# The end of the first part of a fused attention and MLP backward kernel: order of the last two tiles

## The chip, the cores and the metric

The kernel runs on one core of one Trainium2 chip. The metric is the device time of one execution in microseconds (us). A core has TensorE (PE in the profile, with its weight loads as PEld), VectorE (DVE), ScalarE (ACT), GpSimd (POOL) and SyncE (SP, which here only issues DMAs). Every engine works through its own instructions in the order in which the program lists them, and instructions of different engines wait for each other through semaphores.

## What is computed

The reference is a block with attention (32 heads of 16) times a gate, and its gradients. S is 2048, D is 512, F is 1792. Cut to what matters:

```
xn = layernorm(x)                       # A_x
s  = attention(layernorm-ed x) @ wo
y  = layernorm(xn)
m  = gelu(y @ w1 + b1) @ w2 + b2
g  = silu(m)
out = x + s * g
# returned: out and the gradients of A_x, wqkv, wo, w1, b1, w2, b2 for a given grad_out
```

For this case only a few of the backward values count. With sg = sigmoid(m) the gate is G = m * sg, its derivative times grad_out is B = (sg + (1 - sg) * G) * grad_out, and the gradient that goes into the output projection is dso = grad_out * G. The gradient of the attention's output is dO = dso @ wo^T. G and B ("gbr"), and dso ("dsr"), are stored to DRAM for the last part; dO is needed by attention's backward in two layouts.

## The kernel before

The program has three parts. The first (class Pre, lines 102 to 469) makes everything that attention reads: the norms, q, k, v, the hidden layer of the MLP, the gate and dO. The second (attention_core) runs attention forward and backward in one sweep of 64 blocks of 16 steps, one step for each 128 keys. The third (class Grads) makes the weight gradients and the gradient of x.

The work is scheduled by hand: the order in the code is the order on every engine. Rows are handled in 16 tiles t of 128 rows. The loop at lines 425 to 457 runs over t; in each turn it works on four different tiles at different stages:

- gate(t), lines 363 to 378: PE multiplies 14 times for m (ps_m, L367), DVE adds the bias (L373), ACT takes a tanh (L374), DVE makes sg, G and dso from it (L375, L376, L377; "the gate chain" below). It hands back a function for gate_b, four POOL instructions that make B (L381 to L384). For t below 14 the loop calls it at once; for 14 and 15 it is put into the list lastb.
- dproj(t - 2), lines 389 to 394: PE makes dO of an older tile (ps_do, L392), DVE copies it to SBUF (nat, L393), POOL copies it again into another layout (ND, L394).
- t_do(t - 3): PE transposes that dO (tp_ps, L173), ACT copies the result (dOT, L177). t_ds(t - 1): the same for dso (dsoT, L177), which dproj of that tile will read.
- after(t) for every fourth tile: SP stores ND and dOT to DRAM (L403, L404) and loads from there what attention's first pair of heads needs ("do", L95 and L98), which waits for the store. gate_store(t) for every second tile: SP stores gbr and dsr of two tiles (L409, L410).

After the loop, lines 458 to 469 finish tiles 13 to 15: dproj(14), t_do(13), t_ds(15), t_do(14), dproj(15), t_do(15), after(15), then both functions in lastb on POOL, and gate_store(15) with POOL as the queue that issues its two DMAs.

In turn t = 15, line 446 is a one-element Exp on ACT. Its purpose is the load of the table that Exp needs (ACT_TABLE_LOAD) ahead of attention's first exp.

Behind lastb, POOL's next instructions are the memsets of a second set of attention operands (make_op, L47 to L50), then small copies and loads in the steps of attention.

A step g of attention has on PE: scores s (L1082) and d (L1104), the transposes tT of an older step (L1166), the products X (L1196, L1199, L1203) and, from step 20, Z (L1280). ACT takes the exp (L1091) and copies tT into ek (L1178). DVE multiplies d by the exp into gts (L1121) and copies a small share of ek (L1178). SP transposes every pair of steps of gts by DMA into gk (L1137); there are four gts tiles of two steps each. An ek tile holds four steps.

The first part's tiles give their SBUF to the tiles of attention. Tile pools with reuse_waits="tile" make the first write into a new tile wait for the last use of the old tiles that lay in the same bytes, a DMA that reads them included. The tile gd (sg, m and dsr of the last tiles, lines 341 and 342) and the tiles gbr and dOT lie in that region, and ek tiles come to lie there.

The functions that the change touches:

Of the kernel before, what the change touches and what calls it, by code (L numbers as in the profile page):

```python
# [10 lines left out]
ACT = mybir.ActivationFunctionType  # L11
ALU = mybir.AluOpType
# [4 lines left out]
NT = S // 128  # L17
# [84 lines left out]
class Pre:  # L102


    def __init__(self, ctx, tc, k, op0, A_x, A_wqkv, A_wo, B_w1, B_b1, B_w2, B_b2, grad_out):
        nc = tc.nc
# [27 lines left out]
        b2bc = sm.tile([128, D], bf16, name="b2bc")  # L134
# [10 lines left out]
        ld = nc.sync.dma_start  # L145
# [24 lines left out]
        def tp(src, dst, e):  # L170
            pt = psT.tile([128, IC, 128], bf16, name="tp_ps", tag="tp")
            for b in range(IC):
                nc.tensor.transpose(pt[:, b, :], src(b), k.ident_bf[:])  # L173
            if e:
                nc.vector.tensor_copy(out=dst, in_=pt[:])
            else:
                nc.scalar.copy(out=dst, in_=pt[:])  # L177
# [52 lines left out]
        def stores_nat(gq):  # L230
            g = gq % 2
            t0 = gq * 4
            ld(out=k.NAT_s[:, :, t0:t0 + 4, :].rearrange("a p t c -> p a t c"), in_=NS[:, g].rearrange("p a t j c -> p a t (j c)"))
            ld(out=k.NATQq_s[:, :, t0:t0 + 4, :].rearrange("a p t c -> p a t c"), in_=NQ[:, g].rearrange("p a t j c -> p a t (j c)"))
# [11 lines left out]
        def wkv_rows(ic):  # L246
            arr = yr[:, 2 * (ic % 2):2 * (ic % 2) + 2, :].rearrange("p x d -> p (x d)").rearrange("p (r h e) -> p r h e", r=8, h=4)
            for e0, f0 in ((0, 2 * D), (16, D)):
                nc.gpsimd.tensor_copy(out=arr[:, :, :, e0:e0 + 16],
                                      in_=wqkv_sb[:, ic, f0:f0 + D].rearrange("p (r h e) -> p r h e", r=8, h=4))  # L250
            nc.gpsimd.dma_start(out=k.WKV_s[ic * 128:ic * 128 + 128, :], in_=arr.rearrange("p r h e -> p (r h e)"))
# [18 lines left out]
        def bound():  # L270
            nc.vector.tensor_reduce(out=kmx[:, 4:5], in_=kmx[:, 0:4], axis=AX.X, op=ALU.max)
            nc.vector.tensor_scalar(out=kmx[:, 5:6], in0=kmx[:, 4:5], scalar1=UINFL, scalar2=None, op0=ALU.mult)
            nc.scalar.activation(out=UT, in_=qn2[:], func=ACT.Sqrt, scale=kmx[:, 5:6])
            ld(out=k.UT_s[:, :], in_=UT)
# [64 lines left out]
        gbr = mid.tile([128, 4, 2, D], bf16, name="gbr", tag="m2")  # L339
        dOT = mid.tile([128, 2, IC, 512], bf16, name="dOT", tag="m3")  # L340
        gd = mid.tile([128, 8, D], bf16, name="gd", tag="m4")
        gw, dsr = gd[:, 0:4, :], gd[:, 4:8, :]
# [6 lines left out]
        def hid(g, fc):  # L349
            ps = psA.tile([128, 512], f32, name="ps_h1", tag="mm")  # L350
            for ic in range(IC):
                nc.tensor.matmul(ps[:], lhsT=w1_sb[:, ic, fc * 128:(fc + 1) * 128], rhs=yT[:, ic, g * 512:(g + 1) * 512],  # L352
                                 start=(ic == 0), stop=(ic == IC - 1))
            nc.scalar.activation(out=hgT[:, g % 2, fc, :], in_=ps[:], func=ACT.Gelu_apprx_tanh, bias=b1c[:, fc:fc + 1], scale=1.0)
            i = (g * 7 + fc // 2) % 3
            nc.vector.tensor_scalar(out=h1r[:, i, fc % 2, :], in0=ps[:], scalar1=b1c[:, fc:fc + 1], scalar2=None, op0=ALU.add)
            if fc % 2 == 1:
                ld(out=h1v[:, fc - 1:fc + 1, g * 512:(g + 1) * 512], in_=h1r[:, i])
            if fc in (6, 13):
                c0 = fc - 6  # L360
                ld(out=hgv[:, c0:c0 + 7, g * 512:(g + 1) * 512], in_=hgT[:, g % 2, c0:c0 + 7, :])

        def gate(t):
            g, t4 = t // 4, t % 4
            ps = psA.tile([128, 512], f32, name="ps_m", tag="mm")
            for fc in range(FC):
                nc.tensor.matmul(ps[:], lhsT=hgT[:, g % 2, fc, t4 * 128:(t4 + 1) * 128], rhs=w2_sb[:, fc, :],  # L367
                                 start=(fc == 0), stop=(fc == FC - 1))
            dot = dotr[:, g % 2, t4, :]
            m_, sg = gw[:, 2 * (t % 2), :], gw[:, 2 * (t % 2) + 1, :]  # L370
            ta = tau[:]
            G_, B_ = gbr[:, t % 4, 0, :], gbr[:, t % 4, 1, :]
            nc.vector.tensor_tensor(out=m_, in0=ps[:], in1=b2bc[:], op=ALU.add)  # L373
            nc.scalar.activation(out=ta, in_=m_, func=ACT.Tanh, scale=0.5)  # L374
            nc.vector.tensor_scalar(out=sg, in0=ta, scalar1=0.5, scalar2=0.5, op0=ALU.mult, op1=ALU.add)  # L375
            nc.vector.tensor_tensor(out=G_, in0=m_, in1=sg, op=ALU.mult)  # L376
            nc.vector.tensor_tensor(out=dsr[:, t % 4, :], in0=dot, in1=G_, op=ALU.mult)  # L377
            return lambda: gate_b(B_, G_, sg, dot)

        def gate_b(B_, G_, sg, dot):  # L380
            nc.gpsimd.tensor_scalar(out=B_, in0=sg, scalar1=-1.0, scalar2=1.0, op0=ALU.mult, op1=ALU.add)  # L381
            nc.gpsimd.tensor_tensor(out=B_, in0=B_, in1=G_, op=ALU.mult)
            nc.gpsimd.tensor_tensor(out=B_, in0=B_, in1=sg, op=ALU.add)
            nc.gpsimd.tensor_tensor(out=B_, in0=B_, in1=dot, op=ALU.mult)  # L384

        def t_ds(t):
            tp(lambda b: dsr[:, t % 4, b * 128:(b + 1) * 128], dsoT[:, t % 2], 0)

        def dproj(t):
            ps = psA.tile([128, 512], f32, name="ps_do", tag="mm")  # L390
            for bc in range(IC):
                nc.tensor.matmul(ps[:], lhsT=dsoT[:, t % 2, bc, :], rhs=woT[:, bc, :], start=(bc == 0), stop=(bc == IC - 1))  # L392
            nc.vector.tensor_copy(out=ndc[:, t % 2, :], in_=ps[:])  # L393
            nc.gpsimd.tensor_copy(out=ND[:, (t // 4) % 2, :, t % 4, :], in_=ndc[:, t % 2, :].rearrange("p (a c) -> p a c", a=NPAIR))  # L394

        def t_do(t):
            g = (t // 4) % 2
            tp(lambda b: ndc[:, t % 2, b * 128:(b + 1) * 128], dOT[:, g, :, (t % 4) * 128:(t % 4) * 128 + 128], 0)

        def after(t):  # L400
            if t % 4 == 3:
                g = t // 4
                ld(out=k.NATQd_s[:, :, g * 4:g * 4 + 4, :].rearrange("a p t c -> p a t c"), in_=ND[:, g % 2])  # L403
                ld(out=k.DOT_s.rearrange("(c p) s -> p c s", p=128)[:, :, g * 512:(g + 1) * 512], in_=dOT[:, g % 2])  # L404
                op0["do"](g)

        def gate_store(t, ld=ld):
            if t % 2 == 1:
                ld(out=k.GB_s.rearrange("(t p) x d -> p t x d", p=128)[:, t - 1:t + 1], in_=gbr[:, (t - 1) % 4:(t - 1) % 4 + 2])  # L409
                ld(out=k.DSO_s.rearrange("(t p) d -> p t d", p=128)[:, t - 1:t + 1], in_=dsr[:, (t - 1) % 4:(t - 1) % 4 + 2, :])  # L410

        def load_dot(g):
            ld(out=dotr[:, g % 2], in_=go2[:, g * 4:g * 4 + 4])

        lastb = []
# [9 lines left out]
        for t in range(NT):  # L425
            g, t4 = t // 4, t % 4
            n0, n1 = (0, 4, 8, 11, 14)[t4:t4 + 2]
            if g < 3:
                for fc in range(n0, n1):
                    hid(g + 1, fc)  # L430
            if t == 4:
                op0["q"]()
            if t >= 1:
                gate_store(t - 1)
            if t == 0:
                bound()
            gb = gate(t)
            if t == 0:
                stores_nat(3)
            if t < 14:  # L440
                gb()
            else:
                lastb.append(gb)
            if t == 15:

                nc.scalar.activation(out=b2bc[0:1, 0:1], in_=b2bc[0:1, 0:1], func=ACT.Exp)
            if t >= 2:
                dproj(t - 2)
            if t >= 3:
                t_do(t - 3)  # L450
                after(t - 3)
            if t >= 1:
                t_ds(t - 1)
            if t4 == 3 and g + 2 < 4:
                load_dot(g + 2)
            if 2 <= t < 6:
                wkv_rows(t - 2)
        dproj(NT - 2)
        t_do(NT - 3)
        after(NT - 3)  # L460
        t_ds(NT - 1)
        t_do(NT - 2)
        after(NT - 2)
        dproj(NT - 1)
        t_do(NT - 1)
        after(NT - 1)
        for gb in lastb:
            gb()
        gate_store(NT - 1, nc.gpsimd.dma_start)


GA = 0.044715
# [993 lines left out]
```

## Time and profile before

| what | value |
|---|---|
| median of 3 runs | 2246.61 us (2244.68 to 2248.53) |
| span of the profiled execution, first to last instruction | 2242.4 us |
| median of the runs less that span | 4.2 us |
| PE, DVE, ACT, POOL busy in the span | 2160.1, 1912.2, 1734.5, 606.8 us |
| last matmul group of gate(15), L367 | starts at 207.0 us |
| last copy of dO by DVE, L393 | starts at 220.2 us |
| attention's first exp, L1091 | starts at 221.9 us |
| gate_b of tiles 14 and 15 on POOL, L381 to L384 | 221.6 to 230.2 us |
| table load, L446 | 1.28 us, and 0.20 us for the Exp behind it |

The page gives the span of the profiled execution and no other time of it, so the runs' median is the only figure for what lies around the span. Times within the profile are counted from the span's start. A line of a timeline reads: start, duration, engine, line of the kernel, operation, what is written and read, shape, count, and in brackets how long the engine stood idle before it and what ended that. A granted clock of 0.50 means that PE ran at half speed. A chain of waits reads: start, duration, who.

### The profile page before, as it was taken

To read this page: it belongs to the slowest core of one execution; us is meant where nothing else is said; L and a number is where in the kernel's file an instruction comes from. 1 tells how busy PE (TensorE), PEld (TensorE's weight loads), DVE (VectorE), ACT (ScalarE), POOL (GpSimd) and SP (SyncE) were. 2 spreads that over 40 slices of the span, in tenths; PEclk is the share of its full clock that TensorE was granted. 3 is DMA by queue.
4 is the path that set the end of the run, shared out by engine and by line. 5 is a ranking of instruction groups with operands and counts; after the bars stand their busy time and mean duration, and the time that the engine had idled before them with its cause. 6 is when DMAs were issued, how large, how long until landed. Compare 5 with 4: busy or idle time off the path is not lost.

```text
span 2242.4 us, 74217 instructions
## 1 busy us (share of the span) xinstructions
PE 2160.1 (96%) x30690; PEld 1205.0 (54%) x30690; DVE 1912.2 (85%) x3626; ACT 1734.5 (77%) x2481; POOL 606.8 (27%) x1387
## 2 busy tenths in 40 slices
PE   6998999999999999999999999999999999989996
PEld 3444555555555555555555555555555554434443
DVE  6676799999999999999999999999999997777623
ACT  4764788888888888888888888888888886674213
POOL 4276413122222222131222222221312224310012
PEclk9999899999999999999999999999999999999998
DMA  7786999999999999999999999999999999899972
GB/s 238 242 273 197 184 199 194 202 200 203 195 203 194 200 197 206 196 199 200 198 203 197 203 192 204 199 199 197 204 196 190 204 205 273 194 257 240 233 222 94
DMA packets 1421747, 461.15 MB, mean 206 GB/s; under 512 B 1334622, under 2 KB 1405662, under 8 KB 1421408
## 3 DMA queue, kind: packets, MB, share of 16 engines
q1 hardware_dynamic: 1406880, 424.67, 99.3%
q0 software_dynamic: 12944, 30.16, 5.4%
q8 instruction: 240, 3.93, 0.8%
q10 hardware_dynamic: 1584, 1.57, 0.2%
q14 instruction: 99, 0.81, 0.1%
HBM read 62.79 MB, written 64.75 MB: 57 GB/s over the span
## 4 chain that ended last, share of the span: by engine, by line
PE 86%; DMA 5%; DVE 2%; issue 2%; ACT 2%; POOL 2%; SPq 0%; POOLq 0%; DVEq 0%; ACTq 0%
PE tT L1166 23%; PE d L1104 14%; PE X L1196 10%; PE Z L1280 10%; PE X L1199 5%; PE X L1203 5%; PE s L1082 2%; PE ps_m L367 2%; PE ps_dy L902 2%; PE ps_dw L973 2%; PE ps_dh L868 2%; PE ps_h L352 2%; DMA out_dram<-ot 2%; PE XT L1222 1%; PE ps_dwkv L820 1%
## 5 line engine op out<-in xcount | busy, mean ns | idle before, releaser
L1121 DVE TENSOR_TENSOR gts<-d,ets 128x512 bf16<-128x512 f32 x2048 | 1363.2, 684 | 101.0 <-ACT ek L1178 20.3
L1091 ACT ACTIVATE ets<-s 128x1024 bf16<-128x1024 f32 x1024 | 1048.7, 1024 | 198.5 <-PE s L1082 95.2
L1166 PE MATMUL tT<-ident_bf,ets 128*128 128x128 bf16 x7168 | 568.9, 219 | 16.7 <-ACT ek L1178 6.9
L1166 PEld LDWEIGHTS <-ets 128*128 128x128 bf16 x7168 | 445.5, 97 | 242.0 <-issue 240.2
L1178 ACT COPY ek<-tT 128x448 f32<-128x448 f32 (+2 forms) x1024 | 501.6, 490 | 8.1 <-DVE ek L1178 6.9
L1104 PE MATMUL d<-QDT,KVT 32*128 32x512 bf16 x2048 | 458.6, 385 | 0.0
L1082 PE MATMUL s<-QDT,KVT 32*128 32x512 bf16 x2048 | 401.6, 381 | 3.4 <-ACT ets L1091 3.2
L1104 PEld LDWEIGHTS <-KVT 32*128 32x128 bf16 x2048 | 145.4, 91 | 323.9 <-issue 323.9
L1196 PE MATMUL X<-ets,NAT 128*32 128x256 bf16 x4096 | 300.6, 284 | 0.1
L1203 PE MATMUL X<-gts,NAT 128*17 128x256 bf16 x4096 | 290.0, 273 | 0.0
L1199 PE MATMUL X<-ets,Lc 128*32 128x256 bf16 x4096 | 289.9, 273 | 0.0
L1340 POOL COPY tick<-gts 1x2 bf16<-1x2 bf16 x205 | 36.2, 176 | 606.1 <-DVE gts L1121 606.1
L1280 PE MATMUL Z<-gk,W 128*32 128x512 bf16 x2048 | 197.8, 379 | 1.0 <-DVE acc L1294 1.0
L1280 PE MATMUL Z<-ek,W 128*32 128x512 bf16 x1792 | 198.6, 379 | 0.0
L1245 POOL TENSOR_TENSOR W<-NATQq,rL 128x128 bf16<-128x128 bf16 x64 | 25.4, 397 | 526.1 <-DVE rL L1244 443.3
L1196 PEld LDWEIGHTS <-NAT 128*32 128x32 bf16 x4096 | 106.2, 93 | 110.8 <-issue 11.4
L1082 PEld LDWEIGHTS <-KVT 32*128 32x128 bf16 x2048 | 139.0, 91 | 12.5 <-issue 9.5
L1178 DVE COPY ek<-tT 128x64 f32<-128x64 f32 (+1 forms) x576 | 132.4, 230 | 5.5 <-POOL KVT L50 4.2
L1280 PEld LDWEIGHTS <-W 128*32 128x32 bf16 x4096 | 109.7, 97 | 11.4 <-issue 1.5
L1199 PEld LDWEIGHTS <-Lc 128*32 128x32 bf16 x4096 | 107.9, 96 | 0.0
L1203 PEld LDWEIGHTS <-NAT 128*17 128x17 bf16 x4096 | 103.6, 92 | 3.1
L1280 PE MATMUL Z<-ekd,W 128*32 128x512 bf16 x256 | 97.0, 379 | 0.0
(244 smaller groups left out, 2339.3 us busy)
## 6 DMA issues: line engine op xcount, KB each, us to landing
gk<-gts SPq DMA_TRANSPOSE x512, 5.1
H1T_s<-h1r SPq DMA_DIRECT2D x28, 256.0 KB, 4.3
HGT_s<-hgT SPq DMA_DIRECT2D x8, 896.0 KB, 4.6
DH_s<-stg SPq DMA_DIRECT2D x12, 512.0 KB, 3.1
hch<-DH_s SPq DMA_DIRECT2D x12, 512.0 KB, 4.7
gp<-H1T_s SPq DMA_DIRECT2D x9, 512.0 KB, 5.4
out_dram<-ob_w POOLq DMA_DIRECT2D x36, 128.0 KB, 4.1
NAT_s<-NS SPq DMA_DIRECT2D x4, 1056.0 KB, 6.2
```

What stands on the lines that cost most here:

```text
L352: nc.tensor.matmul(ps[:], lhsT=w1_sb[:, ic, fc * 128:(fc + 1) * 128], rhs=yT[:, ic, g * 512:(g + 1) * 512], start=(ic == 0), stop=(ic == I ...
L367: nc.tensor.matmul(ps[:], lhsT=hgT[:, g % 2, fc, t4 * 128:(t4 + 1) * 128], rhs=w2_sb[:, fc, :], start=(fc == 0), stop=(fc == FC - 1))
L1082: nc.tensor.matmul(s[:, hj, :], lhsT=op["KVT"][r:r + 32, kb * 128:(kb + 1) * 128], rhs=op["QDT"][r:r + 32, qc * 512:(qc + 1) * 512], start ...
L1091: nc.scalar.activation(out=st_et[g][:, :, :, a[1] % 4, :].rearrange("k b h q -> k h b q"), in_=cur["s"][:].rearrange("k h (b q) -> k h b q ...
L1104: nc.tensor.matmul(d[:], lhsT=op["KVT"][r:r + 32, kb * 128:(kb + 1) * 128], rhs=op["QDT"][r:r + 32, qc * 512:(qc + 1) * 512], start=True, ...
L1121: nc.vector.tensor_tensor(out=gts[:, kb % 2, hj, :].rearrange("k (b q) -> k b q", b=4), in0=st_d.pop((g, hj))[:].rearrange("k (b q) -> k b ...
L1166: nc.tensor.transpose(t[:, i, :], et[:, b // 2, b % 2, kk, :], ident_bf[:])
L1178: copy(out=blk[j]["Ek"][kb // 4][:, kb % 4, lo:hi].rearrange("q i k -> q (i k)").bitcast(f32), in_=st_T[g][:, lo:hi].rearrange("q i k -> q ...
L1196: nc.tensor.matmul(X[r:r + 32, 0:256], lhsT=NATt[:, kb, hj, 1:33], rhs=ev, start=(kb == 0), stop=False, skip_group_check=True, tile_positi ...
L1199: nc.tensor.matmul(X[r:r + 32, 256:512], lhsT=Lc[:], rhs=ev, start=False, stop=False, skip_group_check=True, tile_position=(0, r))
L1203: nc.tensor.matmul(X[r:r + 17, 256:512], lhsT=NATt[:, kb, hj, 0:17], rhs=gv, start=False, stop=(kb == 15), skip_group_check=True, tile_pos ...
L1280: nc.tensor.matmul(Z[r:r + 32, :], lhsT=WT[j % 2][1 - part][:, qb, hj, :], rhs=mv, start=(part == 0 and qb == 0), stop=(part == 1 and qb = ...
```

## The change

It rearranges the end of the first part. In words:

- In turn 15 the gate chain (L375 to L377) comes after dproj(13), so DVE's copy of that older dO stands ahead of it. All other turns keep their order.
- The one-element Exp moves from turn 15 to a place after t_ds(15), behind the copy of dsoT(15) on ACT.
- After the loop the order is now: gate_b(14) on POOL, t_do(13), t_ds(15), the store of dsr(14, 15) by SP, the Exp, dproj(14), dproj(15), t_do(14), t_do(15), gate_b(15) on DVE, after(15). The calls after(13) and after(14), which did nothing, are gone.
- gate_b(15) is made by DVE instead of POOL, the same four instructions.
- The store of gbr(14, 15) is issued by SP within after(15), behind the stores of ND and dOT and ahead of the loads "do" of group 3. The two stores were issued by POOL, gbr first.

```diff
@@ -372,16 +372,20 @@
             G_, B_ = gbr[:, t % 4, 0, :], gbr[:, t % 4, 1, :]
             nc.vector.tensor_tensor(out=m_, in0=ps[:], in1=b2bc[:], op=ALU.add)
             nc.scalar.activation(out=ta, in_=m_, func=ACT.Tanh, scale=0.5)
-            nc.vector.tensor_scalar(out=sg, in0=ta, scalar1=0.5, scalar2=0.5, op0=ALU.mult, op1=ALU.add)
-            nc.vector.tensor_tensor(out=G_, in0=m_, in1=sg, op=ALU.mult)
-            nc.vector.tensor_tensor(out=dsr[:, t % 4, :], in0=dot, in1=G_, op=ALU.mult)
-            return lambda: gate_b(B_, G_, sg, dot)
-
-        def gate_b(B_, G_, sg, dot):
-            nc.gpsimd.tensor_scalar(out=B_, in0=sg, scalar1=-1.0, scalar2=1.0, op0=ALU.mult, op1=ALU.add)
-            nc.gpsimd.tensor_tensor(out=B_, in0=B_, in1=G_, op=ALU.mult)
-            nc.gpsimd.tensor_tensor(out=B_, in0=B_, in1=sg, op=ALU.add)
-            nc.gpsimd.tensor_tensor(out=B_, in0=B_, in1=dot, op=ALU.mult)
+
+            def chain():
+                nc.vector.tensor_scalar(out=sg, in0=ta, scalar1=0.5, scalar2=0.5, op0=ALU.mult, op1=ALU.add)
+                nc.vector.tensor_tensor(out=G_, in0=m_, in1=sg, op=ALU.mult)
+                nc.vector.tensor_tensor(out=dsr[:, t % 4, :], in0=dot, in1=G_, op=ALU.mult)
+            if t < NT - 1:
+                chain()
+            return chain, lambda e: gate_b(e, B_, G_, sg, dot)
+
+        def gate_b(e, B_, G_, sg, dot):
+            e.tensor_scalar(out=B_, in0=sg, scalar1=-1.0, scalar2=1.0, op0=ALU.mult, op1=ALU.add)
+            e.tensor_tensor(out=B_, in0=B_, in1=G_, op=ALU.mult)
+            e.tensor_tensor(out=B_, in0=B_, in1=sg, op=ALU.add)
+            e.tensor_tensor(out=B_, in0=B_, in1=dot, op=ALU.mult)
 
         def t_ds(t):
             tp(lambda b: dsr[:, t % 4, b * 128:(b + 1) * 128], dsoT[:, t % 2], 0)
@@ -397,17 +401,24 @@
             g = (t // 4) % 2
             tp(lambda b: ndc[:, t % 2, b * 128:(b + 1) * 128], dOT[:, g, :, (t % 4) * 128:(t % 4) * 128 + 128], 0)
 
-        def after(t):
+        def after(t, f=lambda: None):
             if t % 4 == 3:
                 g = t // 4
                 ld(out=k.NATQd_s[:, :, g * 4:g * 4 + 4, :].rearrange("a p t c -> p a t c"), in_=ND[:, g % 2])
                 ld(out=k.DOT_s.rearrange("(c p) s -> p c s", p=128)[:, :, g * 512:(g + 1) * 512], in_=dOT[:, g % 2])
+                f()
                 op0["do"](g)
 
-        def gate_store(t, ld=ld):
+        def gate_store(t):
             if t % 2 == 1:
-                ld(out=k.GB_s.rearrange("(t p) x d -> p t x d", p=128)[:, t - 1:t + 1], in_=gbr[:, (t - 1) % 4:(t - 1) % 4 + 2])
-                ld(out=k.DSO_s.rearrange("(t p) d -> p t d", p=128)[:, t - 1:t + 1], in_=dsr[:, (t - 1) % 4:(t - 1) % 4 + 2, :])
+                gb_store(t)
+                dso_store(t)
+
+        def gb_store(t):
+            ld(out=k.GB_s.rearrange("(t p) x d -> p t x d", p=128)[:, t - 1:t + 1], in_=gbr[:, (t - 1) % 4:(t - 1) % 4 + 2])
+
+        def dso_store(t):
+            ld(out=k.DSO_s.rearrange("(t p) d -> p t d", p=128)[:, t - 1:t + 1], in_=dsr[:, (t - 1) % 4:(t - 1) % 4 + 2, :])
 
         def load_dot(g):
             ld(out=dotr[:, g % 2], in_=go2[:, g * 4:g * 4 + 4])
@@ -434,18 +445,17 @@
                 gate_store(t - 1)
             if t == 0:
                 bound()
-            gb = gate(t)
+            chain, gb = gate(t)
             if t == 0:
                 stores_nat(3)
             if t < 14:
-                gb()
+                gb(nc.gpsimd)
             else:
                 lastb.append(gb)
-            if t == 15:
-
-                nc.scalar.activation(out=b2bc[0:1, 0:1], in_=b2bc[0:1, 0:1], func=ACT.Exp)
             if t >= 2:
                 dproj(t - 2)
+            if t == NT - 1:
+                chain()
             if t >= 3:
                 t_do(t - 3)
                 after(t - 3)
@@ -455,18 +465,18 @@
                 load_dot(g + 2)
             if 2 <= t < 6:
                 wkv_rows(t - 2)
+        lastb[0](nc.gpsimd)
+        t_do(NT - 3)
+        t_ds(NT - 1)
+        dso_store(NT - 1)
+
+        nc.scalar.activation(out=b2bc[0:1, 0:1], in_=b2bc[0:1, 0:1], func=ACT.Exp)
         dproj(NT - 2)
-        t_do(NT - 3)
-        after(NT - 3)
-        t_ds(NT - 1)
+        dproj(NT - 1)
         t_do(NT - 2)
-        after(NT - 2)
-        dproj(NT - 1)
         t_do(NT - 1)
-        after(NT - 1)
-        for gb in lastb:
-            gb()
-        gate_store(NT - 1, nc.gpsimd.dma_start)
+        lastb[1](nc.vector)
+        after(NT - 1, lambda: gb_store(NT - 1))
 
 
 GA = 0.044715
```

## The prediction

> **What bounds the kernel now.** I read the page first: PE is busy 96% of the span and the chain that ended last is 86% PE, so over the whole kernel any gain must come from a place where PE stands still. The 40 slices show one early on (PE at 8 tenths in the fourth, 168 to 224 us, PEclk at 8 in the fifth), so I took the busy time by windows, then the waits, the chain and the timeline between 203 and 250 us. This is the seam between the first part and attention. In the waits of DVE there:
> ```profile
> DVE ek L1178 <- POOL KVT L50: 4.2, 1, 4.2
> ```
> One wait of 4.2 us, before the first VectorE copy into the second ek tile (step 4 of attention). The chain of waits tells what led to it:
> ```profile
> 220.98 0.62 POOL ND L394
> 221.59 0.60 POOL gbr L381
> ...
> 230.48 0.46 POOL GB_s L409
> 231.27 5.95 DMA DSO_s<-gd
> 237.40 0.24 DVE ek L1178
> ```
> POOL does the eight gate_b instructions of tiles 14 and 15 only after the last ND copy (221.6 to 230.2), then issues the two gate stores, and the second lands at 237.22. The ek copy starts 0.18 later: gd's bytes belong to the attention pools by then. The two views name different releasers (a memset of POOL ended at about 237.3 too); both stand behind the same POOL list. What it costs is read from the exps, one a step:
> ```profile
> 232.57 1.02 ACT L1091 ACTIVATE ets<-s 128x1024 bf16<-128x1024 f32 x1
> ...
> 238.07 1.03 ACT L1091 ACTIVATE ets<-s 128x1024 bf16<-128x1024 f32 x1
> 240.50 1.02 ACT L1091 ACTIVATE ets<-s 128x1024 bf16<-128x1024 f32 x1 [0.60 <-PE s L1082]
> 242.67 1.02 ACT L1091 ACTIVATE ets<-s 128x1024 bf16<-128x1024 f32 x1 [0.60 <-PE s L1082]
> 244.17 1.02 ACT L1091 ACTIVATE ets<-s 128x1024 bf16<-128x1024 f32 x1
> ```
> Steps take 1.50 to 1.56 us around them. These take 5.50, 2.43 and 2.17, so the stall costs 3.95 + 0.88 + 0.62 = **5.5 us**. The last two are the clock (columns: busy us of PE, PEld, DVE, ACT, POOL, then granted clock, DMA share, GB/s):
> ```profile
> 218.97:222.39 3.42, 1.76 (x11) 0.65 (x12) 0.69 (x1) 1.59 (x4) 1.33 (x3) 1.00 0.04 10
> 222.39:225.80 3.41, 1.73 (x13) 0.78 (x13) 2.50 (x4) 2.02 (x3) 3.25 (x3) 0.50 1.10 305
> ...
> 232.63:236.04 3.41, 1.41 (x23) 0.82 (x23) 0.54 (x1) 0.96 (x1) 3.41 (x3) 1.00 1.14 341
> 236.04:239.46 3.42, 1.23 (x15) 0.92 (x18) 1.71 (x5) 1.44 (x3) 3.25 (x3) 0.50 0.09 25
> 239.46:242.87 3.41, 3.41 (x41) 1.50 (x32) 2.23 (x5) 2.15 (x4) 0.65 (x2) 0.50 1.21 244
> ```
> A stretch of 3.41 us with PE about half idle is followed by one at half clock.
>
> **Start of attention, step by step.** The first exp is at 221.89 now.
>
> *Table load.* It takes 1.28 + 0.20 us on ACT between tanh(15) and the copies dOT(12), dsoT(14). PE waits 3.2 us for dsoT(14). Gone from there, dsoT(14) is ready at 214.1 instead of 215.6. The load now follows dsoT(15) (217.4 below) and ends at 218.9, before dOT(14) is wanted at 219.9: hidden; if that cover went, at most 1.5.
>
> *Gate chain behind dproj(13).* The older copy of dO (L393, 0.68) follows L373(15) directly, at 212.3 to 213.0. It fits in the 0.83 that DVE now waits for tanh. PE does t_do(13) at once. But POOL copies ND(13) at 213.0 and goes straight on with gate_b(14), so the chain L375 to L377 of tile 15, alone before, now runs beside POOL. What that costs:
> ```profile
> 207.69 1.15 POOL L383 TENSOR_TENSOR gbr<-gbr,gd 128x512 bf16<-128x512 bf16 x1
> ...
> 207.92 1.21 DVE L375 TENSOR_SCALAR gd<-tau 128x512 bf16<-128x512 f32 x1 [0.83 <-ACT tau L374]
> ...
> 213.20 0.43 DVE L375 TENSOR_SCALAR gd<-tau 128x512 bf16<-128x512 f32 x1 [0.83 <-ACT tau L374]
> ```
> Beside POOL the instruction ends 0.29 after POOL's (208.84 to 209.13); alone it takes 0.43. The next five of DVE between 203 and 211 end 0.27 to 0.29 behind a POOL instruction too. So L375 ends behind ND(13) (213.64) at 213.9, L376 behind L381(14) (214.5) at 214.8, L377 behind L382(14) (215.75) at **216.0**, instead of 214.5. A loss of 1.5.
>
> *PE.* t_ds(15) stands ahead of dproj(14) and waits for L377: 216.1. The stretch before is idle, so I take half clock as now: four transposes 0.63 (row 217.71), dproj(14) 1.8 (row 215.60: 1.89), dproj(15) 1.1, its dsoT copied by ACT meanwhile, ready at 217.4. That ends at 219.5. The copy nat(15) runs 219.6 to 220.3, t_do(15) starts at 220.4, and the first exp follows 0.92 behind as now (220.97 to 221.89): 221.3, say 221.4. **Gain 0.5 us**: the two dprojs back to back win some 2 us and the port takes 1.5 of them. Bounds: with the chain as fast as alone and full clock (dproj 1.05) the exp starts at about 218.7, gain 3.2; with each of the three waiting 1.26 for POOL (row L376), the start is 0.5 later than now.
>
> *gate_b(15) on DVE*, four instructions after nat(15). The first (tensor_scalar, 0.43) goes ahead of ND(15); the second ends 0.28 behind ND(15), 221.6; two more of 0.42 end at 222.5. The first multiply L1121 comes 1.06 behind the exp, 222.5: hidden, by a hair. POOL's list is short now, so its memsets (1.82, 1.83, 1.8, 1.8; now 232.0 to 239.1) run from 221.4, beside the last two. Does a memset hold DVE?
> ```profile
> 5.16 3.65 POOL L50 MEMSET KVT<- 1x2048 bf16 x2
> ...
> 6.73 0.16 DVE L190 TENSOR_TENSOR lnv<-lnv,rstd 128x2 f32<-128x2 f32 x1
> 7.41 1.55 DVE L195 TENSOR_SCALAR xt<-xt,mv,rstd 128x512 bf16<-128x512 bf16 x1
> ```
> The tensor_scalar was held (1.55, elsewhere 0.38 to 0.41), the tensor_tensor was not. Beside a POOL copy at 20.17 the like tensor_tensor took 0.41. The last three are tensor_tensor, so I take no cost; the other end, held by two memsets, is +2.9, all three by memsets +3.9. The Trainium skill, "SBUF", Who interferes with whom, has the two-input instruction contend only with POOL instructions that read SBUF; its rows here are of 2 elements, and by that page the cost is nothing for 512 too.
>
> **The stall.** dso_store(15) is issued by SP behind do(2), whose last load ends at 218.48. Such stores land after 3.1 to 5.9 us: 221.6 to 224.4. gb_store(15) follows the DOT store (now 222.10 to 222.99) in the 3.3 us in which SP waits for its landing anyway; so do(3) is not later. It lands by 228.3 (5.3 at most). gate_b(14) ends on POOL at 218.2, and the first of the L50 memsets at about 226.7. The ek copy asks 11.3 behind the first exp: 232.7. Everything that either view names is over 4.4 us or more before, and the **5.5 us go in full**; this holds whichever of them was the releaser. Next in line are the gk transposes on SP (a rival). Nothing gives it back later: after 260 us DVE's and PE's waits are some 0.2 us each, and the transposes wait for gts 524 us in all between 300 and 1600, so the queue has room.
>
> **Sum.** 0.5 + 5.5 = 6.0. The profiled execution: span 2242.4 to 2236.4. The page gives no time beside the span; the median of the runs, 2246.61, stands 4.2 above it, taken as what lies around it. So 2246.6 - 6.0 = **2240.6**. The runs before spread by 3.9, which is how the clock stretches fall.
>
> **Rivals.**
> (A) *The port takes the place of the stall*: the DVE chain is held by POOL's memsets ahead of the first multiply. +3.9 against the start, 5.5 gained, the clock perhaps 0.5 of it: 2244 to 2245, middle 2244.5. For it: L195 above, and by the order, POOL is free just then. Against: L190.
> (B) *The transposes become the bound* (slower). The first two gk transposes held SP 3.4 and 4.2 us; the 4.2 us stall gave the queue time. Steps of 1.5 make one due every 3.0 us, and the four gts tiles (two steps each) let DVE run eight steps ahead. If each took 4.2, plus 0.35 for the ekd ones, the lag grows 1.5 a pair of steps, passes the slack at the third, and by step 24 has cost 8: 2246.6 - 6.0 + 8 = 2248.6. It decides from about 2.65 us each. Against: the ten between 227 and 262 have a median of 2.17, and the 4.2 stood beside the gate stores, which are gone by then.
> (C) *The change does not reach the wait*: another landing holds ek. Only the start's 0.5 stays: 2246.1. Little speaks for it, since all named ones are earlier.
> (D) *The dprojs run at full clock*, since PE idles only 2.6 us (213.5 to 216.1) where it idled 3.15: dproj(14) in 1.05 for 1.89 ends the pair 0.9 earlier, 2239.7. Against: the stretch 218.97 to 222.39 had PE busy for 1.76 of 3.42 and half clock followed. The Trainium skill, "TensorE: Matmul & The Clock Gate", Part 1 (What's actually happening), has half clock come after at least one idle window of some 3.4 us, so by that page an idle of 2.6 would keep full clock; the row just named disagrees with it.
>
> **Chances.** Forecast 0.60 (own range 2238.5 to 2242.6), D 0.10, A 0.17, B 0.06, C 0.07. The low end is 3.2 + 5.5 = 8.7 gained, 2237.9, rounded to 2238.0; the high end takes in A: 2245.8. A 0.2% difference (4.5 us) is about what a measurement of this kernel can tell from no change: faster means below 2242.1, D and nearly all of the forecast, 0.66; slower is B and a share of C's spread, 0.07; within 0.27.
>
> **What would show it.** Right: no wait of more than 0.5 us at ek L1178 near 232 us; DSO_s issued by SP near 218.5; exps 1.5 apart from the fifth step and no half clock after about 230; L377's last at 216; first exp near 221.4. Wrong: DVE L381 to L384 each over 1 us ahead of the first L1121 (A); waits of gts on a DMA in the first 24 steps (B); the ek wait still there under another name (C); or the first exp later than 221.9.

## The result and the profile after

The changed kernel takes **2240.25 us** (median of 9 runs, 2236.51 to 2243.41), the kernel before, run beside it, 2246.46 (9 runs, 2242.73 to 2249.24). The ratio is **0.9973**, with a 95% interval of 0.9963 to 0.9984: 6.1 us gained, between 3.6 and 8.3. The prediction was 2240.6, 6.0 gained.

The profiled execution of after has a span of 2234.6 us in a time of 2236.51, its fastest run, so the two spans differ by 7.75, more than the medians. Where those 7.75 lie is read from five marks in the two traces: the start of the last group of ps_m products (gate(15), L367), ahead of which nothing of this seam was changed; the first exp of attention; the sixteenth exp after it; the last exp; the end.

| stretch | before, us | after, us | gained |
|---|---|---|---|
| start to the last ps_m group | 207.02 | 206.39 | 0.64 |
| that group to the first exp | 14.87 | 14.19 | 0.68 |
| first exp to the exp 16 steps on | 31.59 | 26.41 | **5.18** |
| from there to the last exp | 1616.87 | 1615.32 | 1.55 |
| last exp to the end | 372.01 | 372.30 | -0.29 |

Two rows answer to the change: 0.68 at the start and 5.18 in the first steps, **5.9 together**. The others hold the same code. From here on "+x" means x us after the start of that last ps_m group, so that traces can be laid over one another; "first 16 steps" is the third row.

**The stall.** The exps of the same steps, in the timeline of ACT after the change (start, duration):
```profile
229.89 1.02 ACT L1101 ACTIVATE ets<-s 128x1024 bf16<-128x1024 f32 x1
...
231.40 1.02 ACT L1101 ACTIVATE ets<-s 128x1024 bf16<-128x1024 f32 x1
...
232.90 1.02 ACT L1101 ACTIVATE ets<-s 128x1024 bf16<-128x1024 f32 x1
...
234.40 1.02 ACT L1101 ACTIVATE ets<-s 128x1024 bf16<-128x1024 f32 x1
...
235.90 1.02 ACT L1101 ACTIVATE ets<-s 128x1024 bf16<-128x1024 f32 x1
```
They are 1.50 apart. The step of 5.5 and the two at half clock behind it are gone. In the timeline of DVE the first copy into the second ek tile stands at 232.03, with no wait in front of it:
```profile
232.03 0.23 DVE L1188 COPY ek<-tT 128x64 f32<-128x64 f32 x1
```

**The start.** In the chain of waits (start, us, what was run or waited for) from the gate chain to the first exp:
```profile
214.07 1.27 DVE gd L379
215.33 0.05 issue
215.38 0.61 PE tp_ps L173 x4
215.99 2.83 PE ps_do L396 x8
...
218.91 0.70 DVE nat L397
...
219.66 0.41 PE tp_ps L173 x4
...
220.57 1.04 ACT ets L1101
```
The gate chain of tile 15 ends at 215.33 (+8.94; the diff makes the prediction's L377 into L379), the eight products of both dprojs follow back to back, and the first exp comes at +14.19 where it came at +14.87. DVE's last gate instruction took three times what it takes alone (1.26 to 0.42). The timeline of DVE and POOL says why:
```profile
212.98 0.78 POOL L385 TENSOR_SCALAR gbr<-gd 128x512 bf16<-128x512 bf16 x1
...
213.32 0.71 DVE L378 TENSOR_TENSOR gbr<-gd 128x512 bf16<-128x512 bf16 x1
...
213.85 1.20 POOL L386 TENSOR_TENSOR gbr<-gbr 128x512 bf16<-128x512 bf16 x1
214.07 1.26 DVE L379 TENSOR_TENSOR gd<-dotr,gbr 128x512 bf16<-128x512 bf16 x1
...
220.22 1.81 POOL L47 MEMSET KVT<- 128x2048 bf16 x1
...
220.59 0.42 DVE L387 TENSOR_TENSOR gbr<-gbr,gd 128x512 bf16<-128x512 bf16 x1
...
221.05 0.42 DVE L388 TENSOR_TENSOR gbr<-gbr,dotr 128x512 bf16<-128x512 bf16 x1
221.64 1.39 DVE L1131 TENSOR_TENSOR gts<-d,ets 128x512 bf16<-128x512 f32 x2 [0.17 <-ACT ets L1101]
```
L378 ends 0.27 behind POOL's L385, L379 0.28 behind L386. L377 (0.80 us) does the same behind POOL's copy ND(13), which ran from 212.40 to 213.02. L387 and L388, beside a memset of POOL, take 0.42. The first multiply (L1131) then waits for the exp alone.

### The profile page after: what moved, and what is told of

Same layout as the page of the kernel before. It is cut to its first block, busy times and chain, and to the rows that moved or that the text cites. A ratio compares the mean times of both kernels' runs of the same rounds, so it can differ in the third digit from the quotient of the medians.

```text
span 2234.6 us, 74214 instructions
## 1 busy us (share of the span) xinstructions
PE 2159.7 (97%) x30690; PEld 1204.5 (54%) x30690; DVE 1914.0 (86%) x3630; ACT 1734.3 (78%) x2481; POOL 601.6 (27%) x1381
## 4 chain that ended last, share of the span: by engine, by line
PE 90%; DMA 3%; DVE 2%; ACT 2%; issue 1%; POOL 1%; SPq 0%; POOLq 0%; DVEq 0%; ACTq 0%
PE tT L1176 24%; PE d L1114 15%; PE X L1206 10%; PE Z L1290 10%; PE X L1209 5%; PE X L1213 5%; PE s L1092 3%; PE ps_m L367 2%; PE ps_dy L912 2%; PE ps_dw L738 2%; PE ps_dw L983 2%; PE ps_dh L878 2%; PE ps_h L352 2%; DMA out_dram<-ot 2%; PE XT L1232 1%
## 5 line engine op out<-in xcount | busy, mean ns | idle before, releaser
L1131 DVE TENSOR_TENSOR gts<-d,ets 128x512 bf16<-128x512 f32 x2048 | 1363.2, 684 | 98.3 <-ACT ek L1188 18.3
L1092 PEld LDWEIGHTS <-KVT 32*128 32x128 bf16 x2048 | 138.8, 91 | 11.8 <-issue 8.8
```

The costliest lines, as they stand in the source:

```text
L1092: nc.tensor.matmul(s[:, hj, :], lhsT=op["KVT"][r:r + 32, kb * 128:(kb + 1) * 128], rhs=op["QDT"][r:r + 32, qc * 512:(qc + 1) * 512], start ...
L1131: nc.vector.tensor_tensor(out=gts[:, kb % 2, hj, :].rearrange("k (b q) -> k b q", b=4), in0=st_d.pop((g, hj))[:].rearrange("k (b q) -> k b ...
```

## Experiments

Two theories of the stall: **L**, the landing of the store of dsr (gd's bytes, the DSO store) holds the second ek tile; **M**, the wait's other name, the L50 memset of POOL. Of the start: **P**, the deferred chain pays for POOL's gate_b(14) beside it. The first four kernels ran beside the kernel before at a median of 2248.33 (19 runs), the last four at 2247.94 (17 runs). Runs of one kernel spread by some 7 us and more. In the ten traces the fourth row of the table, steps far inside attention, takes 1615 to 1624 us, so single times decide nothing here; the marks in the traces do.

### e1: before, with the dsr store alone moved
```diff
         t_ds(NT - 1)
+        dso_store(NT - 1)
...
-        gate_store(NT - 1, nc.gpsimd.dma_start)
+        gb_store(NT - 1, nc.gpsimd.dma_start)
```


> The kernel before with one edit: the store of dsr(14, 15) is issued by SP behind t_ds(15) instead of by POOL behind the gate_b list; all else, gate_b on POOL and the gbr store on POOL included, stays. Theory L (the landing of the dsr store held the first VectorE copy into the second ek tile): the store lands near 222 to 224, POOL's last gate_b ends near 230, the copy asks near 233, so its wait of 4.2 us is gone, the first 16 steps take about 26.4 us instead of 31.6, the start (last ps_m group to first exp, 14.9 us) is as before, and the time is 5 to 5.5 us lower, 2241. Rival M (the memset of POOL that the waits view names): POOL saves only one DMA issue of 0.73 us, so the wait shrinks from 4.2 to about 3.5 and the time falls by less than 1 us.

The timeline from 231 us on (POOL, ACT, DVE):
```profile
231.99 0.79 POOL L413 DMA_DIRECT2D GB_s<-gbr  x1 [0.30 <-POOL gbr L384]
...
232.78 1.82 POOL L47 MEMSET KVT<- 128x2048 bf16 x1
...
234.52 1.83 POOL L48 MEMSET QDT<- 128x2048 bf16 x1
234.75 0.23 DVE L1185 COPY ek<-tT 128x64 f32<-128x64 f32 x1
...
236.27 1.79 POOL L50 MEMSET KVT<- 1x2048 bf16 x1
```
The gate derivatives are still made late on POOL, the gbr store is issued at 231.99 and lands at 235.62, and the memset ends later still. The ek copy runs at 234.75, ahead of both, with a wait of 0.09. The first 16 steps take 26.28 (before 31.59), the start is unchanged (+14.81). Ratio 0.9982 (0.9971 to 0.9993; 10 runs): 4.0 us, 1.6 to 6.5. **One store, issued early by SP, takes away the whole stall.** The gbr store and the memset hold nothing.

### e2: before, with the two gate stores of POOL swapped
```diff
-        gate_store(NT - 1, nc.gpsimd.dma_start)
+        dso_store(NT - 1, nc.gpsimd.dma_start)
+        gb_store(NT - 1, nc.gpsimd.dma_start)
```


> The kernel before with the two POOL stores in the other order: dsr first, gbr second. Theory L: dsr is issued at about 230.5 instead of 231.3 and is not behind the gbr store's data; it lands 3.9 to 5.9 us later, at 234.4 to 236.4, and the ek copy starts right behind it, 0.8 to 2.8 us earlier than before: wait 1.4 to 3.4. Rival M: POOL's list is as long as before, the memset ends at the same point, wait 4.2.

```profile
230.25 0.79 POOL L416 DMA_DIRECT2D DSO_s<-gd  x1
231.04 0.73 POOL L413 DMA_DIRECT2D GB_s<-gbr  x1
...
233.42 0.22 DVE L1185 COPY ek<-tT 128x64 f32<-128x64 f32 x1 [0.15 <-PE tT L1173]
...
235.25 1.79 POOL L50 MEMSET KVT<- 1x2048 bf16 x1
```
The ek copy starts at 233.42, 0.25 behind the landing of DSO (233.17), and 1.8 ahead of that memset's start. M falls here a second time: same memsets, same two stores, other order. The size was missed. A wait of over a us was expected; it was 0.15, and the first 16 steps took 26.49. The DMA issues of 228 to 240 us (KB, us from issue to landing) show the reason:
```profile
GB_s<-gbr POOLq DMA_DIRECT2D x1, 512.0 KB, 6.5
DSO_s<-gd POOLq DMA_DIRECT2D x1, 256.0 KB, 2.9
```
In front, the dsr store lands after 2.9 us, where 3.9 to 5.9 were expected; behind the gbr store it took 5.9 before. The start was also late (+15.71 for +14.87, two half-clock stretches in a row), so the copy asked 0.8 later, which hides as much of the wait. The time was 2247.82 (one run): besides the late start, its steps after the sixteenth took 1624 us, as in e1, for 1617 before. Only the seam is read.

### e3: the changed order without the early derivatives and the early store
```diff
-        lastb[0](nc.gpsimd)
...
-        dso_store(NT - 1)
...
-        lastb[1](nc.vector)
-        after(NT - 1, lambda: gb_store(NT - 1))
+        after(NT - 1)
+        for gb in lastb:
+            gb(nc.gpsimd)
+        gb_store(NT - 1, nc.gpsimd.dma_start)
+        dso_store(NT - 1, nc.gpsimd.dma_start)
```


> The changed kernel with gate_b(14), gate_b(15) and both stores put back on POOL behind the last ND copy, as before; the new order of the rest, the deferred gate chain and the late table load stay. Theory L: the stall at the second ek tile is back, about 4 us of wait and 5.5 us in all; the gate chain of tile 15 runs without POOL beside it, so L379 ends 1.5 us earlier than in the changed kernel and the first exp comes 13.0 us or less behind the last ps_m group (14.2 in the changed kernel, 14.9 before). Sum: 1.5 to 2 us below before, about 4 above the changed kernel. Rival O (the order, not the stores, is what the change wins): the time stays near that of the changed kernel, 6 below before.

The stall is back (waits of DVE; then, from the chain of waits, the store and the copy behind it):
```profile
DVE ek L1189 <- POOL KVT L50: 4.0, 1, 4.0
```
```profile
227.80 5.80 DMA DSO_s<-gd
...
233.88 0.23 DVE ek L1189
```
First 16 steps 31.62. The waits view names the memset again, the chain the store; e1 and e2 say which is right. And the gate chain, with POOL idle once its copy ND(13) is done:
```profile
212.65 0.61 POOL L398 COPY ND<-nat 128x512 bf16<-128x512 bf16 x1 [0.58 <-DVE nat L397]
...
212.74 0.80 DVE L377 TENSOR_SCALAR gd<-tau 128x512 bf16<-128x512 f32 x1 [0.16 <-ACT tau L374]
...
213.58 0.42 DVE L378 TENSOR_TENSOR gbr<-gd 128x512 bf16<-128x512 bf16 x1
214.04 0.42 DVE L379 TENSOR_TENSOR gd<-dotr,gbr 128x512 bf16<-128x512 bf16 x1
```
L378 and L379 take 0.42 each, the chain ends at +7.81 for +8.94 in after: **gate_b(14) beside the chain costs 1.1 us**, as P has it. This kernel's dprojs ran at full clock too, and the first exp came at +11.80, 2.4 earlier than in after: 1.1 from the chain, 1.3 from the clock. Against before the start is 3.1 shorter, and the stall stays, so rival O is out. Ratio 0.9990 (0.9976 to 1.0003; 10 runs): 2.2 us, between 5.4 gained and 0.7 lost.

### e4: after, with the gate chain of tile 15 not deferred
```diff
-            if t == NT - 1:
-                chain()
```
and gate() runs its chain at once for every tile.

> The changed kernel with the gate chain of tile 15 back in its old place, ahead of DVE's copy of dproj(13). Theory P (the port between DVE and POOL eats the deferral): POOL gets the ND copy of tile 13 and gate_b(14) only after the chain, so the chain runs alone, L379 ends about 1.5 us earlier, but t_do(13) waits for the later copy and holds t_ds(15) behind it: t_ds(15) near 8.6 us behind the start of the last ps_m group instead of 9.0, first exp 0.4 us earlier than in the changed kernel. Rival (the deferral is what shortens the start): the first exp comes about 1 us or more later than in the changed kernel.

The chain ended at +7.50 and t_ds(15) at +8.39, 0.6 ahead of after (+8.99). The dprojs ran at full clock and the first exp came at +12.53. Even with the 1.3 us added that full clock was worth in e3, that is ahead of after's +14.19, so the rival, which has it about 1 us later, is out. The deferral by itself still wins: where the deferred chain has no gate_b(14) beside it (e3, e5), t_ds(15) starts at +7.87, 0.5 ahead of here. As the change has it, it loses 0.6. And the later gate_b(14) on POOL now stood beside gate_b(15) on DVE:
```profile
219.33 1.32 DVE L385 TENSOR_TENSOR gbr<-gbr 128x512 bf16<-128x512 bf16 x1
220.69 0.71 DVE L386 TENSOR_TENSOR gbr<-gbr,gd 128x512 bf16<-128x512 bf16 x1
221.44 0.71 DVE L387 TENSOR_TENSOR gbr<-gbr,dotr 128x512 bf16<-128x512 bf16 x1
222.08 2.47 DVE L1128 TENSOR_TENSOR gts<-d,ets 128x512 bf16<-128x512 f32 x4
```
L385 ends 0.27 behind POOL's L387; L386 and L387 stand beside POOL's two ND copies. The first multiply came at +14.77, 2.24 behind the exp (1.06 in after). So the gain at the multiply is 0.48 against after (+15.25), less than at the exp. It is not the last word: 16 steps on the exp is 1.9 ahead of after's (12.53 + 26.14 for 14.19 + 26.41), in part by the clock, since half clock in attention lasted 3.4 us here and 6.8 there. One run, 2236.7.

### e5: after, with POOL waiting for the chain
```diff
+        nc.gpsimd.tensor_copy(out=b1_bf[0:1, 0:2], in_=dsr[0:1, 3, 0:2])
         lastb[0](nc.gpsimd)
```


> The changed kernel with one POOL instruction more: a copy of two elements of dsr(15) ahead of gate_b(14), so that POOL starts gate_b(14) only when the gate chain of tile 15 is done. Theory P (POOL beside the chain costs the start 1.1 to 1.5 us): the chain ends 7.8 us behind the start of the last ps_m group (8.9 in the changed kernel), the first exp comes at 11.8 with the dprojs at full clock or 12.9 at half (14.2). But gate_b(14) now lies beside gate_b(15) on VectorE, so the first multiply comes more than the usual 1.06 behind the exp, at about 14 (15.25). No wait at the second ek tile. Rival (the chain is slow by itself): no change at L379, 14.2 and 15.25.

The chain ran without gate_b(14) beside it (L379 in 0.42, end +7.80, t_ds(15) +7.86) and the first exp came at +11.79, the dprojs at full clock. The contention moved:
```profile
219.44 1.15 POOL L388 TENSOR_TENSOR gbr<-gbr,dotr 128x512 bf16<-128x512 bf16 x1
...
219.55 1.33 DVE L386 TENSOR_TENSOR gbr<-gbr 128x512 bf16<-128x512 bf16 x1
```
The first multiply came at +14.01, 2.2 behind its exp. The first 16 steps took 27.00, 0.6 more than in after; 0.5 of it is the thirteenth exp, which stands behind a DMA transpose (see rival B below). One run, 2243.05. Both e4 and e5 say: **gate_b(14) on POOL holds VectorE wherever it lies beside its instructions on SBUF data**, before t_ds(15) or before the first multiply. What that costs is not the same: 16 steps on the exp is still 1.8 ahead of after's, at the same 6.8 us of half clock in attention, so the delay of the multiply is not passed on in full.

### e6: after, with the table load back in its old place
```diff
         ... turn 15, behind gate(t)
+            if t == NT - 1:
+                nc.scalar.activation(out=b2bc[0:1, 0:1], in_=b2bc[0:1, 0:1], func=ACT.Exp)
...
-        nc.scalar.activation(out=b2bc[0:1, 0:1], in_=b2bc[0:1, 0:1], func=ACT.Exp)
```


> The changed kernel with the one-element Exp back in turn 15, behind tanh(15) on ACT. dsoT(14) is ready 1.5 us later, at about 8.5 us behind the start of the last ps_m group, but t_ds(15) stands ahead of dproj(14) on PE and waits for the gate chain until 9.0. Theory: no effect, first exp at 14.2, first multiply at 15.25, within 0.3 but for the clock. Rival (moving the table load off dsoT(14) is what shortened the start): the first exp 1.5 us later, 15.7.

```profile
213.10 1.28 ACT L456 ACT_TABLE_LOAD   x1
...
214.97 0.57 ACT L177 COPY dsoT<-tp_ps 128x512 bf16<-128x512 bf16 x1
```
The copy dsoT(14), which dproj(14) needs, waits for the load and ends at 215.54 (+8.51). PE goes on with t_ds(15) at +8.97 all the same, since that waits for L379. First exp +14.16, first multiply +15.22 (after +14.19 and +15.25). **The move of the table load is worth nothing here.** Where the chain ends at +7.8, as in e8, a dsoT(14) at +8.51 would be the later of the two; no run tests that. One run, 2240.44.

### e7: after, with gate_b(15) on POOL
```diff
-        lastb[1](nc.vector)
+        lastb[1](nc.gpsimd)
```


> The changed kernel with gate_b(15) on POOL behind the last ND copy instead of on VectorE. POOL ends it about 18.2 us behind the start of the last ps_m group; SP then issues the gbr store about 3 us later than in the changed kernel and the loads behind it at nearly the same time, since these wait for the DOT store until about 18.6. Theory (VectorE was free there, so this part of the change neither wins nor costs): first multiply at 15.25, no wait at ek, first 16 steps 26.4 us, all within 0.3. Rival (gate_b must leave POOL for the stall to go): a wait of 1 us or more at an ek tile in the first 16 steps.

No wait at ek (0.03), though the gbr store is issued only at 224.82; first multiply +15.10. The first 16 steps took 25.56, less than after's 26.41 by the clock alone: its half clock at the start of attention lasted 3.4 us instead of 6.8. VectorE's four instructions are worth nothing. One run, 2239.11.

### e8: after's order and early dsr store; gate derivatives late on POOL
```diff
-        lastb[0](nc.gpsimd)
...
-        lastb[1](nc.vector)
-        after(NT - 1, lambda: gb_store(NT - 1))
+        after(NT - 1)
+        for gb in lastb:
+            gb(nc.gpsimd)
+        gb_store(NT - 1, nc.gpsimd.dma_start)
```


> The new order with gate_b(14) and gate_b(15) on POOL behind the last ND copy and the gbr store on POOL behind them, as before, but the dsr store by SP early, as in the changed kernel. If both theories hold (the dsr store's landing made the stall, POOL beside the gate chain costs the start), it has the start of the order-only kernel, first exp 11.8 us behind the last ps_m group (12.9 at half clock), the multiply 1.06 behind, and the 26.4 us of the changed kernel for the first 16 steps: 1.3 to 2.4 us below the changed kernel, 7.5 to 8.5 below before. If gate_b on VectorE or the gbr store by SP is needed, a wait at an ek tile comes back and the time is above the changed kernel's.

A smaller change that has both gains. Timeline:
```profile
218.41 0.38 SPq L421 DMA_DIRECT2D DSO_s<-gd  x1
...
228.86 0.79 POOL L418 DMA_DIRECT2D GB_s<-gbr  x1 [0.30 <-POOL gbr L388]
...
231.66 0.23 DVE L1189 COPY ek<-tT 128x64 f32<-128x64 f32 x1 [0.16 <-PE tT L1177]
```
The gbr store lands at 232.67, a us after the ek copy it does not hold. First exp +13.44 (11.8 was expected at full clock, 12.9 at half), first multiply +14.50, both 0.75 ahead of after. The chain was 1.1 ahead (+7.80); the rest went to the clock, since the eight products of the dprojs stand in the timeline of PE with 3.58 us here and 3.02 in after, where half clock ended at 218.06, ahead of the last of them. First 16 steps 26.31. Ratio 0.9966 (0.9955 to 0.9977; 12 runs), 7.6 us (5.1 to 10.1). The expectation of 1.3 to 2.4 below after was too high: the interval overlaps that of after, so the 0.75 is shown by the trace alone; the time does not separate the two.

## Why the prediction was right, step by step

- **The stall, 5.5 us, goes in full.** Measured 5.18: the three steps of 5.51, 2.43 and 2.17 became 1.50 each, an earlier one grew from 2.02 to 2.17, and a later one from 1.56 to 1.84 (as in every kernel here without the stall except e2; the cause is open). The prediction left open whether the store or the memset was the releaser. It was the store (e1, e2). Its forecast landing, 221.6 to 224.4, is not confirmed, since the trace of after has no landing for that store; that ek does not wait shows that it came before 232. This is the term that carries the result, and only one part of the change makes it.
- **The gate chain ends 1.5 later, behind POOL.** Right in mechanism: each DVE instruction ended some 0.28 behind its neighbour on POOL. t_ds(15) was put at 216.1, which is +9.08; it came at +8.99. The chain ended 1.4 later than before (+8.94 for +7.52): 1.1 is gate_b(14), the other 0.3 is still there in e3, e5 and e8, where L377 waits for the ND copy alone.
- **The two dprojs win some 2 us, at half clock.** The pair did run at half clock; nat(15), put at 219.6 (+12.58), started at +12.52, the first exp at +14.19 for a predicted +14.38. So the start won 0.68 where 0.5 was forecast. With gate_b(14) out of the way (e8) the same order wins 1.43 at half clock, not the some 2 that the working gives it, and the early gate_b(14) took about half of that.
- **The table load is hidden; dsoT(14) is ready 1.5 earlier.** True (the load ran at 216.68 to 217.96, dOT(14) was copied at 219.06), and worth nothing: the sum gave no separate price to that 1.5, and e6 shows that dsoT(14) was not the last thing PE waited for once t_ds(15) stood in front.
- **gate_b(15) on DVE ends at 222.5, beside memsets, hidden.** Right: it ended at 221.47 (+15.08 for a predicted +15.48), and the multiply behind it waited for its exp. But the step was not needed, nor the gbr store by SP (issued at 221.70 in after, at 224.82 in e7, at 228.86 by POOL in e8, without a wait at ek in any).
- **Rival A** (memsets hold DVE): out. The L387 and L388 beside the L47 memset took 0.42, as alone. The rule the prediction took from the Trainium skill ("SBUF", Who interferes with whom) holds here for 512 elements, as it did for the 2 of L190.
- **Rival B** (the gk transposes): out in after. SP waits for gts, not DVE for SP; in the waits of 203 to 250 us after:
```profile
SPq L1147 <- DVE gts L1131: 12.5, 6, 2.8
```
But the queue is not far behind. In e4 and e5, whose attention starts earlier, the thirteenth exp starts 0.1 behind the landing of the first ekd transpose, and that step takes 1.82 and 2.03 us for 1.55; the line is from e4. In after that transpose lands at 239.69, 0.8 ahead of the exp.
```profile
239.44 1.02 ACT L1098 ACTIVATE ets<-s 128x1024 bf16<-128x1024 f32 x1 [0.48 <-DMA ekd<-ets]
```
- **Rival C**: out, the wait is 0.04. **Rival D** (full clock for the dprojs): not met in after, where this half-clock stretch begins at 214.65 (columns as in the prediction):
```profile
211.24:214.65 3.41, 0.97 (x12) 0.62 (x12) 3.18 (x5) 2.08 (x4) 2.75 (x4) 1.00 1.15 312
214.65:218.06 3.41, 2.68 (x10) 1.31 (x11) 0.93 (x2) 1.95 (x3) 2.76 (x3) 0.50 0.40 139
```
It was met in e3, e4 and e5, whose order of PE is the same or nearly so. Half clock is a toss here, worth 1.3 to 1.6 us: t_ds(15) to nat(15) took 2.27 at full clock (e3, e5), 3.53 in after, 3.91 in e8, where half clock lasted over both dprojs.

The sum of 6.0 agreed with the measured 5.9 of the two rows and with the medians' 6.2, but part of that is luck: the terms were +0.2 at the start and -0.3 at the stall. The 4.2 us taken for what lies around the span is too much: time less span is 1.7 to 1.9 in every later run, so the profiled execution of before was some 2 us faster than the median of its runs. The gain does not depend on it.

## What to carry to other kernels

When a first write into reused memory waits, list every reader of the old contents, stores to memory included, and move the one whose end is last; here that was one store, and the rest of the change, as it was made, was worth 0.7 us in the traces. The waits view names one of several semaphores, so a landing and a memset that end together are told apart only by moving one of them. An instruction that POOL does earlier, and that reads SBUF, delayed the VectorE instructions on SBUF data that it then lay beside (here two-input ones and the one-input L377), so look for the place where VectorE has none on the path.

## What the runs showed of the hardware that was not expected

**The clock needs no idle stretch.** Counting PE's busy time in the stretch of 3.41 us just ahead, where that stretch itself ran at full clock: half clock followed on 0.30, 1.41 and 1.76 (before), 0.97 and 1.69 (after), 1.23 (e8), 1.63 (e5), 1.74 (e4) and 1.87 (e3); it did not follow on 1.46, 1.88 and 2.00 (e4), 2.65 (after), 1.76 and 2.27 (e3), 1.93 and 2.10 (e5). In these stretches 1.41 or less always brought it, 1.93 or more never, and between them it went either way; far inside attention one of e6 with 1.99 (935.46 to 938.88) brought it too. Behind a stretch at half clock the count is another: in after 2.13 busy (221.48 to 224.89) were followed by half clock again. The stretches' grid differs from run to run, so the same kind of wait is sometimes split in two: e4's wait of PE for 2.75 us, from 212.72, is split at 213.52 and brings nothing. E4's stretch with 1.46, and the next at full clock:
```profile
213.52:216.93 3.41, 1.46 (x12) 0.76 (x12) 1.82 (x4) 1.83 (x4) 1.37 (x3) 1.00 1.12 309
216.93:220.35 3.42, 2.00 (x16) 0.95 (x16) 2.83 (x4) 2.99 (x6) 3.26 (x4) 1.00 0.28 83
```
The Trainium skill, "TensorE: Matmul & The Clock Gate", Part 1 (What's actually happening), asks for at least one idle window of some 3.4 us; here PE stood still for at most 2.6 us at a time in after and 1.5 in e8, and half clock followed both. The measurements decide.

**The store that stood second on POOL's queue landed late.** The 256 KB dsr store of POOL took 5.9 us (before) and 5.8 (e3) behind the 512 KB gbr store, 2.9 in front of it (e2); the gbr store took 3.6 to 3.9 in front or alone, and 6.5 behind.
